# Windowed attention with block means and a squared-ReLU FFN: the first two chunks in one written order, half of the first chunk's FFN steps as three products

## The chip, the cores and the metric

The kernel runs on one core of one Trainium2 chip. The metric is the device time of one execution in microseconds. A core has TensorE (PE in the profile; its weight loads are PEld), VectorE (DVE), ScalarE (ACT), GpSimd (POOL) and SyncE (SP), which issues every DMA here. Each engine runs its own instructions in the order in which they were written; semaphores join the engines.

## The reference

Four sequences of 768 positions, eight heads of 64, then an FFN over all 3072 rows:

```
k_sum  = max  of k over blocks of 32     # 24 keys per head
v_sum  = mean of v over blocks of 32     # 24 values per head
scores = [ q k^T / 8, kept where |i - j| < 16 ;  q k_sum^T / 8 + log 32 ]
a      = softmax(scores) (sum + 1e-9)
x      = a @ [v ; v_sum]                 # heads side by side: 3072 x 512
r      = max(x @ w_in, 0)                # w_in 512 x 2048
out    = (s * r * r + b) @ w_out         # w_out 2048 x 512, s and b scalars
```

`w_in` and `w_out` come as 64-bit floats. All results are float32.

## The kernel before

**Chunks and steps.** The 3072 rows are cut into 12 chunks of 256. A chunk's attention is worked in four pairs of heads (p = 0 to 3), a pair in two halves of 128 rows. Its FFN is worked in 16 steps (f = 0 to 15): a step is 128 of the 2048 hidden units. Step f has a hidden part (`hidden`: `x @ w_in` into PSUM, 128 x 256), an activation (`activate`: ReLU and square on ACT, `s * r + b` on POOL) and a projection (`project`: two tiles of 128 x 512 that add up over the 16 steps). After the last projection `evict` copies out the chunk.

**Weights.** 32 blocks of 512 KB (an "in" and an "out" block for each step) are loaded as raw 64-bit words once. `scale_weights` (two ACT instructions a block, L118 and L119) and `convert_weights` (DVE, L132 and L134) make float32 of them. In chunk 0 the FFN multiplies in float32. From chunk 1 on, each weight, x and g is split into an upper half that TensorE multiplies in one pass and the rest (`split_weights`: upper half by ACT, lower half by DVE; `activate` splits g on DVE; `attended` splits x), and a product is the sum of three: low x high, high x low, high x high. The weights are split while chunk 0 ends, and stay.

**Attention of one pair.** `scores` (PE), `masked` (DVE: mask, scale, row minimum), `exps` (ACT), `normalize` (DVE), `transposes` (PE), `turned` (ACT copy), `values` (PE), `attended` (ACT copy). The keys and values of a window stand in one tile with 24 columns or rows of block maxima and means behind them: `fill_k` and `fill_v` copy these in (POOL, but DVE for chunk 0). In chunk 0 the scores against the maxima are a matmul of their own (`scores_of_maxima`). The means of the first sequence come from 12 matmul instructions (`mean_of_rows`, L208) against a 0-and-1/32 matrix, and `mean_done` copies them.

**Order.** Everything is written out beforehand into steps of a plan. The start, up to the first steps of chunk 0, is one written list, `FIRST_ORDER`: a letter names the function, a number its pair or step (q: keys and queries of a pair; r: rows of v; v: windows of v; i and o: weight blocks; u: keys and queries of chunk 1; W: dummy matmuls; A and B and D: scaling and converting; S, Z, M, E, N, T, C, V, X: attention; H, J, P: the three parts of an FFN step). After that, formulas place each function. The attention of chunk c lies between the FFN steps of chunk c-1. Chunk 0 takes one hidden part at a time, chunks 1 and 2 two, later ones four; the attention of chunks from 4 on is grouped (all four pairs' scores in a row, then transposes of two pairs, and so on), which `together` decides. The two scalars s and b are loaded by a DMA of their own (`load_scalars`).

**Memory.** Raw weights, split upper halves, and the first loads share 16 slots of 4 KB per partition; converted and lower weights share 33 of 2 KB. PSUM has two buffers each for hidden parts, for projections and for scores, and one each for transposes and for values.

Of the kernel before, what the change touches and what calls it, by code (L numbers as in the profile page):

```python
# [3 lines left out]

# [14 lines left out]
P = 128  # L19
# [17 lines left out]
LAG = 2  # L37
# [7 lines left out]
def windowed_attention_then_relu2_ffn(ctx, tc, qk, vwin, kt, vt, kq, vrow, wp, sb, out):  # L45
# [49 lines left out]
    mean4 = const.tile([P, KR + 20], F32, name="mean4")  # L95
    nc.gpsimd.memset(mean4, 0.0)
    nc.gpsimd.memset(mean4[:, KR - 4 : KR], 1.0 / BLOCK)
    for base, sign in ((0, 1), (BLOCK - 1, -1)):
        nc.gpsimd.affine_select(
            out=mean4[:, KR - 4 : KR], in_=mean4[:, KR - 4 : KR], compare_op=ALU.is_ge, fill=0.0,  # L100
            base=base, pattern=[[-sign * BLOCK, 4]], channel_multiplier=sign,
        )


    w_raw, w_f, w_h, w_l = {}, {}, {}, {}
# [30 lines left out]
    def split_weights(key):  # L136

        name = "_".join(map(str, key))
        whole = w_f.pop(key)
# [3 lines left out]
        nc.scalar.copy(w_h[key], whole)  # L143
        w_l[key] = wring.tile([P, 512], F32R, name=f"wl_{name}", tag="ring")
        nc.vector.tensor_tensor(
            w_l[key], whole, w_h[key].bitcast(F32), ALU.subtract
        )
# [45 lines left out]
    def load_scalars():  # L193
        nc.sync.dma_start(sb_col, sb.partition_broadcast(P))

    def keep_warm(n):

        t = ps_t.tile([P, 4 * P], F32, name="warm", tag="pt")
# [5 lines left out]
    def mean_of_rows(n):  # L204
        if n == 0:
            pm.append(ps_po.tile([P, DM], F32, name="pm", tag="po"))
        for j in (2 * n, 2 * n + 1):
            nc.tensor.matmul(  # L208
                pm[0][:KR], mean4[:, 20 - 4 * j : 20 - 4 * j + KR], vn[n][:, j % 2],
                start=(j == 0), stop=(j == 5),  # L210
            )


    vsum[0] = p2.tile([P, H, D], F32, name="vsum")

    def mean_done():
        nc.scalar.copy(vsum[0][WIN:KR].rearrange("p h d -> p (h d)"), pm[0][WIN:KR])
# [5 lines left out]
    qk_t, vw_t, ps_of, pr_of, mn_of, sm_of, pt_of, pT_of, o_of, xt = ({} for _ in range(10))  # L223
# [7 lines left out]
    def load_unit(c, p):  # L231
        t = p3.tile([P, T + NSUB * KR], F32, name="qk", bufs=4)
        nc.sync.dma_start(t, qk[c - 1, p])
        qk_t[c, p] = t[:, 0:T], t[:, T:].rearrange("p (i k) -> p i k", k=KR)
# [6 lines left out]
    def filler(c):  # L241
        return nc.gpsimd if c else nc.vector

    def fill_k(c, p):
        bi, _ = place(c)
        kw = qk_t[c, p][1]
        filler(c).tensor_copy(kw[:, :, WIN:KR], ksum[bi, p].unsqueeze(1).to_broadcast([P, NSUB, NB]))  # L247

    def fill_v(c, p):
        bi, _ = place(c)  # L250
        for e in range(2):
            filler(c).tensor_copy(  # L252
# [12 lines left out]
    def together(c):  # L265

        return c >= 4

    def scores(c, p, j):
        q, kw = qk_t[c, p]  # L270
        if j == 0:
# [5 lines left out]
            elif p == 2 and together(c):  # L277
# [64 lines left out]
    def turned(c, p):  # L342
# [4 lines left out]
        nc.scalar.copy(pT_of[c, p], pt_of.pop((c, p))[:KR])  # L347

    def values(c, p):
        vw, pT = vw_t.pop((c, p)), pT_of.pop((c, p))  # L350
# [10 lines left out]
        for i in range(NSUB):  # L361
            for e in range(2):
                oi, pi = o[64 * e : 64 * e + 64, i * SUB : (i + 1) * SUB], pT[:, e * T + i * SUB : e * T + (i + 1) * SUB]
                nc.tensor.matmul(oi, vw[:KR, e, i, :], pi, start=True, stop=True)  # L364

    def attended(c, p):
        if p == 0:
            if c == 0:
                xt[c] = (p2.tile([P, NKC, T], F32, name="x", tag="xh"),)
            else:  # L370
                xt[c] = p2.tile([P, NKC, T], F32R, name="xh", tag="xh"), p2.tile([P, NKC, T], F32R, name="xl")
        kcs = slice(p, p + (1 if c < 2 else 2))
        o = o_of.pop((c, p))[:, : (kcs.stop - p) * T].rearrange("p (k t) -> p k t", t=T)
        nc.scalar.copy(xt[c][0][:, kcs], o)
        if c > 0:
            nc.vector.tensor_tensor(xt[c][1][:, kcs], o, xt[c][0][:, kcs].bitcast(F32), ALU.subtract)


    ph_of, ph_both, gg, po = {}, {}, {}, {}

    def hidden(c, f):
        if c < 2 or f % 2 == 0:
            ph_both[0] = ps_h.tile([P, 2, T], F32, name="ph", tag="ph")
        ph = ph_of[c, f] = ph_both[0][:, f % 2]
        if c == 0:
            terms = [(w_f["in", f], xt[c][0], kc) for kc in range(NKC)]
        else:
            xh, xl = xt[c]
            terms = [
                (w["in", f], x, kc) for w, x in ((w_l, xh), (w_h, xl), (w_h, xh)) for kc in range(NKC)  # L390
            ]
# [5 lines left out]
    def activate(c, f):  # L397
        ph = ph_of.pop((c, f))
        r = p2.tile([P, T], F32, name="r")
        nc.scalar.activation(r, ph, AF.Relu)  # L400
        nc.scalar.activation(r, r, AF.Square)  # L401
        if c == 0:
            g = p2.tile([P, T], F32, name="g0", tag="gh", bufs=8)
            nc.gpsimd.tensor_scalar(g, r, s_col, b_col, ALU.mult, ALU.add)  # L404
            gg[c, f] = (g,)
            return
        g = p2.tile([P, T], F32, name="g")
        nc.gpsimd.tensor_scalar(g, r, s_col, b_col, ALU.mult, ALU.add)  # L408
# [6 lines left out]
    def project(c, f):  # L415
        if f == 0:
# [3 lines left out]
        if c == 0:  # L420
            terms = [(g[0], w_f["out", f])]
# [3 lines left out]
        for t in range(T // P):  # L425
            for n, (a, w) in enumerate(terms):
                nc.tensor.matmul(  # L427
                    po[t], a[:, t * P : (t + 1) * P], w,
                    start=(f == 0 and n == 0), stop=(f == NF - 1 and n == len(terms) - 1),
                )  # L430

    def evict(c):
        for t in range(T // P):
            o = stage.tile([P, DM], F32, name="o", tag="stage")
            nc.scalar.copy(o, po[t])  # L435
# [169 lines left out]
```

## Time and profile before

| | us |
|---|---|
| median of three runs | 636.54 (634.94 to 637.05) |
| profiled execution | 637.27 |
| its span, first to last instruction | 635.6 |
| TensorE busy | 625.9 (98%) |
| DVE / ACT / POOL busy | 310.9 / 322.1 / 183.1 |
| first projection begins | 28.72 |
| last matmul ends | 631.92 |
| mean granted clock of TensorE | 0.996 |

The profile's page gives busy time by engine and the chain of work that ended last; further views give the chain in order of time, busy time by stretch of the span, and the instructions of one engine in order of time. A row such as `36.50 1.73 PE ph L393 x8` is start, length, engine, tile written, line, and the number of instructions. A float32 matmul is two instructions. In the views of groups, the numbers behind the bar are busy time, the mean of one in ns, and the engine's idle time before them with who ended it.

### The profile page before, as it was taken

The page shows a single profiled execution, that of the slowest core. Times are in us where ns is not written, and L with a number is a line of the kernel's source. Part 1 is how long each engine was busy: PE and PEld are TensorE (multiplying, and loading weights), DVE is VectorE, ACT ScalarE, POOL GpSimd, SP SyncE. Part 2 cuts the span into 40 slices and gives each one's busy share as a digit, 9 for nine tenths or more (in the row PEclk, how much of TensorE's full clock was granted, in tenths as well). Part 3 has the DMA queues.
Part 4 walks back from the last instruction along what each step waited for, and adds up shares of the span by engine and source line. Part 5 has one row for each costly group of instructions (what it writes and reads, how often), then busy time and mean ns, then how long its engine had stood idle before and what let it go on. Part 6 is the DMA issues. An engine that isn't in the chain of part 4 may idle for free.

```text
span 635.6 us, 14057 instructions
## 1 busy us (share of the span) xinstructions
PE 625.9 (98%) x5188; PEld 548.9 (86%) x5188; DVE 310.9 (49%) x1043; ACT 322.1 (51%) x972; POOL 183.1 (29%) x352
## 2 busy tenths in 40 slices
PE   8799999999999999999999999999999999999997
PEld 6466679989899899899999998998998899899896
DVE  6786758875446245444535226245525424513311
ACT  5999867744537255336426336345346336423321
POOL 3124314323132422422151241151152142232211
PEclk9999999999999999999999999999999999999999
DMA  8999205045104113402601410700520500200000
GB/s 343 387 407 405 107 17 181 2 135 180 50 2 150 47 43 108 162 18 54 211 20 36 145 42 1 270 18 2 176 89 19 178 2 19 84 2 2 34 1 34
DMA packets 27141, 66.40 MB, mean 104 GB/s; under 512 B 3968, under 2 KB 3968, under 8 KB 27072
## 3 DMA queue, kind: packets, MB, share of 16 engines
q1 hardware_dynamic: 27072, 65.50, 29.4%
q8 instruction: 41, 0.67, 0.5%
q14 instruction: 28, 0.23, 0.1%
HBM read 59.05 MB, written 6.29 MB: 103 GB/s over the span
## 4 chain that ended last, share of the span: by engine, by line
PE 95%; DMA 4%; POOL 0%; SPq 0%; issue 0%; ACT 0%; POOLq 0%
PE po L427 43%; PE ph L393 42%; PE pav L364 4%; PE ps L290 3%; PE pt L340 3%; DMA wraw<-in_wp_dram 2%; DMA qk<-in_qk_dram 1%; DMA kq<-in_kq_dram 1%; POOL g L404 0%; SPq L228 0%; ACT o L435 0%; POOL qk L247 0%; POOLq L247 0%
## 5 line engine op out<-in xcount | busy, mean ns | idle before, releaser
L408 POOL TENSOR_SCALAR g<-r,sb_col 128x256 f32<-128x256 f32 x176 | 109.4, 622 | 365.4 <-ACT r L401 253.2
L400 ACT ACTIVATE r<-ph 128x256 f32<-128x256 f32 x192 | 72.7, 378 | 218.3 <-PE ph L393 195.7
L410 DVE CAST gh<-g 128x256 fp32r<-128x256 f32 x176 | 53.3, 303 | 247.8 <-POOL g L408 240.4
L427 PE MATMUL po<-wh,gl 128*128 128x512 f32 x352 | 141.1, 401 | 0.0
L427 PE MATMUL po<-wh,gh 128*128 128x512 f32 x352 | 138.5, 393 | 0.0
L427 PE MATMUL po<-wl_out,gh 128*128 128x512 f32 x352 | 137.4, 390 | 0.0
L393 PE MATMUL ph<-xh,wl_in 128*128 128x256 f32 x704 | 110.2, 279 | 0.0
L393 PE MATMUL ph<-xl,wh 128*128 128x256 f32 x704 | 108.6, 276 | 0.0
L393 PE MATMUL ph<-xh,wh 128*128 128x256 f32 x704 | 108.6, 276 | 0.0
L393 PEld LDWEIGHTS ph<-xh,wl_in 128*128 128x128 f32 x704 | 97.2, 188 | 5.2 <-issue 0.7
L412 DVE TENSOR_TENSOR gl<-g,gh 128x256 fp32r<-128x256 f32 x176 | 81.1, 461 | 31.2 <-PE po L427 14.7
L393 PEld LDWEIGHTS ph<-xl,wh 128*128 128x128 f32 x704 | 93.4, 188 | 0.0
L393 PEld LDWEIGHTS ph<-xh,wh 128*128 128x128 f32 x704 | 92.9, 188 | 0.0
L401 ACT ACTIVATE r<-r 128x256 f32<-128x256 f32 x192 | 80.2, 418 | 6.1
L321 ACT ACTIVATE pr<-pr,mn 128x120 f32<-128x120 f32 x176 | 67.0, 382 | 32.2 <-DVE mn L308 32.1
L427 PEld LDWEIGHTS po<-wh,gh 128*128 128x128 f32 x352 | 66.1, 188 | 14.4
L427 PEld LDWEIGHTS po<-wh,gl 128*128 128x128 f32 x352 | 66.2, 188 | 13.9 <-issue 1.4
L427 PEld LDWEIGHTS po<-wl_out,gh 128*128 128x128 f32 x352 | 66.2, 188 | 13.0
L252 POOL COPY vw<-vsum 24x256 f32<-24x256 f32 x88 | 42.2, 511 | 14.7 <-DMA vsum<-vmean 8.4
L427 PE MATMUL po<-wf_out,g 128*128 128x512 f32 x64 | 31.2, 612 | 3.1 <-POOL g L404 3.1
L435 ACT COPY o<-po 128x512 f32<-128x512 f32 x24 | 14.1, 588 | 39.1 <-PE po L427 36.6
L321 ACT ACTIVATION_READ_ACCUMULATOR pr<-pr,mn 128x1 f32 x176 | 33.0, 187 | 0.0
(70 smaller groups left out, 593.8 us busy)
## 6 DMA issues: line engine op xcount, KB each, us to landing
wraw<-in_wp_dram SPq DMA_DIRECT2D x32, 512.0 KB
qk<-in_qk_dram SPq DMA_DIRECT2D x44, 368.0 KB
vw<-in_vwin_dram SPq DMA_DIRECT2D x48, 256.0 KB
out_dram<-o SPq DMA_DIRECT2D x24, 256.0 KB
kraw<-in_kt_dram SPq DMA_DIRECT2D x12, 384.0 KB
vraw<-in_vt_dram SPq DMA_DIRECT2D x12, 252.0 KB
kq<-in_kq_dram SPq DMA_DIRECT2D x4, 512.0 KB
vraw<-in_vt_dram SPq DMA_DIRECT2D x6, 264.0 KB
```

The source lines that it names most:

```text
L252: filler(c).tensor_copy(vw_t[c, p][WIN:KR, e], vsum[bi][WIN : WIN + NB, 2 * p + e, :].unsqueeze(1).to_broadcast([NB, NSUB, D]),)
L290: nc.tensor.matmul(o, qi, kw[r, i, :], start=True, stop=True)
L321: nc.scalar.activation(pr, pr, AF.Exp, bias=mn_of[c, p][:, n : n + 1], scale=-1.0, accum_out=sm_of[c, p][:, n : n + 1])
L340: nc.tensor.transpose(pt_of[c, p][:KR, n * P : (n + 1) * P], pr[:, n, :], ident)
L364: nc.tensor.matmul(oi, vw[:KR, e, i, :], pi, start=True, stop=True)
L393: nc.tensor.matmul(ph, w[:, kc * P : (kc + 1) * P], x[:, kc], start=(n == 0), stop=(n == len(terms) - 1))
L400: nc.scalar.activation(r, ph, AF.Relu)
L401: nc.scalar.activation(r, r, AF.Square)
L408: nc.gpsimd.tensor_scalar(g, r, s_col, b_col, ALU.mult, ALU.add)
L410: nc.vector.tensor_copy(gh, g)
L412: nc.vector.tensor_tensor(gl, g, gh.bitcast(F32), ALU.subtract)
L427: nc.tensor.matmul(po[t], a[:, t * P : (t + 1) * P], w, start=(f == 0 and n == 0), stop=(f == NF - 1 and n == len(terms) - 1),)
```

## The change

- Eight FFN steps of chunk 0, f = 8 to 15 (`THREE`), are done as three products, so their weights, x and g of chunk 0 are split (`first_upper`, `first_lower`, `split_rows`). Chunk 1 takes its steps in the order 8 to 15, 0 to 7 (`SECOND`).
- Splitting a block is two functions, `upper_weights` (ACT, or DVE with a star) and `lower_weights` (DVE), each in a place of its own.
- The means: each of the six parts is four matmuls of 128 columns that write to four groups of 32 PSUM partitions, one for each pair of heads. They are not copied into chunk 0's windows: `values` multiplies the window alone and `values_of_means` adds a product with the means, whose other rows are zero.
- The scalars ride in two columns behind the first window tile of chunk 1; the load of their own is gone.
- Attention of chunks 2 and 3 is grouped as the later ones; hidden parts of chunk 2 come four at a time.
- `FIRST_ORDER` covers all of chunks 0 and 1, the attention of chunk 2 and the scores of chunk 3. Chunk 1's first scores come before chunk 0's first hidden part, and hidden parts of chunk 1 lie between the projections of chunk 0. Names now carry chunk and pair or step (`H0.9`: hidden part of step 9 of chunk 0); new letters: k and t fill windows, x loads values' windows, y takes the low part of x, Y is one of a hidden part's four products, U the means' product, F the copy of the means, G is `s * r + b`, g splits it, hi, ho, li, lo split weights, O evicts. Stars move work to the other engine: `C*`, `X*`, `hi*`, `ho*`, `G*` run on DVE; `F*` on ACT; `J*` squares on DVE, `J**` takes the maximum there, `J***` both.

```diff
-LAG = 2
...
+    THREE = (8, 9, 10, 11, 12, 13, 14, 15)
+    SECOND = THREE + tuple(f for f in range(NF) if f not in THREE)
+    def steps(c):
+        return SECOND if c == 1 else tuple(range(NF))
...
+    def upper_weights(key, other=False):
         if key[0] == "in":
             pair = slots.tile([P, 2, 512], F32R, name=f"wh_{key[1]}", tag="slot")
             w_h["in", key[1]], w_h["out", key[1]] = pair[:, 0], pair[:, 1]
-        nc.scalar.copy(w_h[key], whole)
...
+        copy(other, w_h[key], whole(key))
+    def lower_weights(key):
+        w_l[key] = wring.tile([P, 512], F32R, name="wl_" + "_".join(map(str, key)), tag="ring")
+        nc.vector.tensor_tensor(w_l[key], whole(key), w_h[key].bitcast(F32), ALU.subtract)
...
-    def load_scalars():
-        nc.sync.dma_start(sb_col, sb.partition_broadcast(P))
+    def scalars():
+        nc.gpsimd.tensor_copy(sb_col, sb_of[0])
...
         for j in (2 * n, 2 * n + 1):
-            nc.tensor.matmul(
-                pm[0][:KR], mean4[:, 20 - 4 * j : 20 - 4 * j + KR], vn[n][:, j % 2],
-                start=(j == 0), stop=(j == 5),
-            )
+            for p in range(NPAIR):
+                nc.tensor.matmul(
+                    pm[0][32 * p : 32 * p + NB], mean4[:, 20 - 4 * j : 20 - 4 * j + NB],
+                    vn[n][:, j % 2, p * P : (p + 1) * P], start=(j == 0), stop=(j == 5),
+                )
...
+    def mean_done(p, other=False):
+        dst = vsum[0][WIN:KR, 2 * p : 2 * p + 2].rearrange("p h d -> p (h d)")
+        src = pm[0][32 * p : 32 * p + NB]
+        copy(not other, dst, src)
...
     def together(c):
-        return c >= 4
+        return c >= 2
...
+    def values_of_means(p):
+        pT, o = pT_of.pop((0, p)), o_of[0, p]
+        for i in range(NSUB):
+            for e in range(2):
+                nc.tensor.matmul(
+                    o[64 * e : 64 * e + 64, i * SUB : (i + 1) * SUB], vsum[0][0:KR, 2 * p + e],
+                    pT[:, e * T + i * SUB : e * T + (i + 1) * SUB], start=False, stop=(i == NSUB - 1),
+                )
...
+                if c == 0:
+                    nc.tensor.matmul(oi, vw[0:WIN, e, i, :], pi[0:WIN], start=(i == 0), stop=False)
+                else:
+                    nc.tensor.matmul(oi, vw[:KR, e, i, :], pi, start=True, stop=True)
...
     def hidden(c, f):
+        if c == 0 and f not in THREE:
+            for kc in range(NKC):
+                hidden_part(f, kc)
+            return
+        xh, xlow = (xt["first"], xl["first"]) if c == 0 else (xt[c], xl[c])
...
+        if other < 2:
+            nc.scalar.activation(r, ph, AF.Relu)
+        else:
+            nc.vector.tensor_scalar(r, ph, 0.0, None, ALU.max)
+        if other % 2:
+            nc.vector.tensor_tensor(r, r, r, ALU.mult)
+        else:
+            nc.scalar.activation(r, r, AF.Square)
...
+        (nc.vector if other else nc.gpsimd).tensor_scalar(g, r_of.pop((c, f)), s_col, b_col, ALU.mult, ALU.add)
...
     FIRST_ORDER = (
...
+        "q1 q0 K0.1 q2 i1 S0.1.0 S0.1.1 W1 q3 Z1 K0.0 M0.1.0 S0.0.0 S0.0.1 Ai1 Z0 M0.1.1 r0 K0.2 M0.0.0 M0.0.1 "
+        "Bi1 W8 E0.0.0 S0.2.0 S0.2.1 u1.1 Z2 u1.0 K0.3 E0.0.1 r1 N0.0 k1.0 S0.3.0 S0.3.1 k1.1 E0.1.0 M0.2.0 r2 "
+        "E0.1.1 T0.0 M0.2.1 Z3 N0.1 v0 E0.2.0 C0.0 E0.2.1 v1 u1.2 i0 S1.0.0 S1.0.1 T0.1 M0.3.0 R0 M1.0.0 k1.2 "
+        "E1.0.0 o3 v2 R1 M1.0.1 N0.2 R2 E1.0.1 S1.1.0 S1.1.1 C0.1* T0.2 E0.3.0 M0.3.1 F0* M1.1.0 E0.3.1 M1.1.1 "
+        "V0.0 F1* F3 U0 N0.3 V0.1 F2 E1.1.0 v3 S1.2.0 S1.2.1 C0.2 i3 T0.3 X0.0 o2 Y1.0 E1.1.1 Ai0 N1.0 U1 M1.2.0 "
+        "V0.2 C0.3 U2 V0.3 U3 N1.1 x1.0 M1.2.1 s0 Ao3 i2 u1.3 X0.1* k1.3 T1.0 Y1.1 Bi0 X0.2 Ai3 Y1.2 o1 X0.3* Xh "
+        "Y1.3 Y0.0 Ao2 Y0.1 o0 D3 Ai2 J0.1*** C1.0* Y0.2 Y0.3 D2 H0.3 G0.1 i4 J0.0* o4 E1.2.0 Ao1 T1.1 Bo1 t1.0 "
+        "o9 Ao0 G0.0 E1.2.1 Bo0 H0.2 S1.3.0 S1.3.1 i9 Ai4 V1.0 Ao4 P0.0 J0.2** X1.0 C1.1* J0.3** Ao9 M1.3.0 x1.1 "
...
+        "G1.6 ho6* H1.4 g1.6 ho1 C2.1 T2.2 G1.2 J1.4** li5 g1.2 H1.1 H1.5 J1.1** G1.1 V2.0 lo7 C2.2* J1.5 V2.2 "
+        "V2.1 V2.3 lo6 S3.2.0 S3.2.1 k3.0 g1.1 S3.3.0 S3.3.1 S3.0.0 S3.0.1 X2.0 lo1 S3.1.0 S3.1.1 P1.1 ho4 g1.7 "
+        "X2.2 P1.2 G1.4 P1.3 y2.0 g1.4 G1.5 y2.2 g1.5 lo4"
     )
...
+    def then(step, order, fn, *args):
+        if (fn, args) not in ahead:
+            at(step, order, fn, *args)
+    for c in range(2, NC):
...
+        then(i - i % 4, HID, hidden, c, f)
+        for stage_of in (activate, scaled, split_rows):
+            then(i, CHAIN, stage_of, c, f)
+        then((i + 4) | 3, PROJ, project, c, f)
```

More of the change, by code (lines that the diff above doesn't have):

```diff
@@ L419, in project @@
         g = gg.pop((c, f))
-        if c == 0:
-            terms = [(g[0], w_f["out", f])]
+        if c == 0 and f not in THREE:
+            terms = [(g[0], whole(("out", f)))]
         else:
@@ new lines, in windowed_attention_then_relu2_ffn, with do @@
+    ahead = set()
+    def do(name):
+        how = {"other": name.count("*")} if name.endswith("*") else {}
+        name = name.rstrip("*")
+        kind = name.rstrip("0123456789.")
+        numbers = tuple(int(x) for x in name[len(kind) :].split(".") if x)
+        if kind in ("hi", "ho", "li", "lo"):
+            ahead.add((upper_weights if kind[0] == "h" else lower_weights, ((side[kind[1]], *numbers),)))
+        else:
+            ahead.add((named[kind], numbers))
+        return named[kind], numbers, how
@@ L533, in windowed_attention_then_relu2_ffn @@
[L533 to L545 removed]
+                        then(base + v_at - 5 + third, LOAD, load_v, bi, p, third)
```

279 lines of the change are left out of this document (126 added, 153 removed), and 19 rows, old and new, of the table FIRST_ORDER.

## The prediction

> **What bounds the kernel now.** I read the page's engine totals and its chain of waits first, then the chain in order of time, then the busy time by stretch, and the rows of single engines for the first 90 us.
>
> ```profile
> span 635.6 us, 14057 instructions
> ...
> PE 625.9 (98%) x5188; PEld 548.9 (86%) x5188; DVE 310.9 (49%) x1043; ACT 322.1 (51%) x972; POOL 183.1 (29%) x352
> ...
> PE 95%; DMA 4%; POOL 0%; SPq 0%; issue 0%; ACT 0%; POOLq 0%
> ```
>
> TensorE is busy for 98% of the span and makes up 95% of the chain that ended last. So time can be won in two ways only: fewer microseconds of matrix work, or less time at the start before that work is dense. The chain in order of time (start, length, what) prices the pieces:
>
> ```profile
> 36.50 1.73 PE ph L393 x8
> ...
> 40.72 1.72 PE po L427 x4
> ...
> 44.16 0.44 PE pt L340 x4
> ...
> 52.26 0.62 PE pav L364 x16
> ...
> 56.90 0.57 PE ps L290 x16
> ...
> 227.47 2.02 PE pav L364 x64
> 229.49 1.80 PE ps L290 x64
> 231.29 5.70 PE po L427 x24
> 236.99 5.47 PE ph L393 x48
> ...
> 253.42 0.87 PE pt L340 x8
> ...
> 279.11 1.80 PE ps L290 x64
> ...
> 631.92 0.59 ACT o L435
> ```
>
> The hidden part of one float32 step is the row with x8 (four products, two instructions each), 1.73 us; its projection (x4) is 1.72; 3.45 together. Four steps with three products cost 5.47 hidden and 5.50 projection (5.70 for the first after attention work), so 2.74 a step. The attention pieces of a chunk run alone cost 0.57 (scores of a pair), 0.44 (transposes), 0.62 (values); a grouped chunk costs 1.80 + 2x0.87 + 2.02 = 5.56. One chunk period is 279.11 - 229.49 = 49.62, and the last matmul ends at 631.92; 3.7 us of output follow.
>
> ```profile
> 0.00:10.00 10.00, 8.19 (x120) 7.09 (x120) 4.23 (x15) 2.98 (x10) 5.34 (x28) 1.00 0.82 306
> 10.00:21.70 11.70, 10.64 (x128) 6.51 (x124) 10.13 (x47) 10.59 (x36) 0.00 (x0) 1.00 1.01 375
> ...
> 40.00:60.00 20.00, 20.00 (x116) 13.06 (x115) 13.19 (x40) 19.81 (x52) 7.48 (x12) 1.00 1.03 405
> ```
>
> The columns of a stretch are its length, then PE, PEld, DVE, ACT and POOL busy time, granted clock, DMA share and GB/s. From 40 to 60 us TensorE has no gap while ACT is at 19.81 of 20 and DVE only at 13.19. So the first chunk is paid in float32 matrix time, ACT is full, DVE has room, and the queue of loads runs at about 405 GB/s.
>
> ```profile
> 28.72 2.71 PE L427 MATMUL po<-wf_out,g 128*128 128x512 f32 x4 [3.10 <-POOL g L404]
> ```
>
> ```profile
> 30.00:32.00 2.00, 2.00 (x14) 0.64 (x16) 1.43 (x3) 1.94 (x4) 0.00 (x0) 0.50 1.03 407
> 32.00:34.00 2.00, 2.00 (x18) 1.50 (x11) 1.53 (x11) 1.95 (x4) 0.00 (x0) 0.69 1.03 405
> ```
>
> TensorE waited 3.10 us for the first g before 28.72, and the granted clock was 0.50 and 0.69 in the four microseconds from 30: (1-0.50)x2 + (1-0.69)x2 = 1.6 us lost.
>
> **Where the two kernels become equal.** I call "the mark" the moment at which the scores of chunk 3 are done and the last four projections of chunk 1 are left. From there both kernels do the same work. In the kernel before, the like moment two chunks later is 231.29, with eight projections left. So the rest after the mark is 631.92 - 231.29 + 2x49.62 - 5.50 = 494.4 us, and the mark of before stands at 631.92 - 494.4 = 137.5. (Chunks 2 and 3 went ungrouped before; their 0.7 us each are inside 137.5 and are gone after.)
>
> **Matrix work up to the mark, part by part.** Hidden: 8 float32 steps x 1.73 and 24 steps (8 of chunk 0, 16 of chunk 1) x 1.37 = 46.7. Projection: 8 x 1.72 and 20 x 1.375 = 41.3. Before, the same were 16 x 1.73 + 16 x 1.37 and 16 x 1.72 + 12 x 1.375 = 93.6; the eight changed steps give 5.6 us back.
>
> ```profile
> L208 PE MATMUL pm<-vn,mean 128*120 128x512 f32 x12 | 5.7, 598 | 0.0
> ```
>
> The block means were 12 instructions of 128x512 for 24 useful rows, 5.7 us. They become 48 of 128 columns in four column groups. No row shows this form. A float32 instruction of 256 columns takes 1.73/8 = 0.216 us, 0.84 ns a column, so 48 x 128 columns take 5.2 us one behind the other and 1.3 four at a time: these are the bounds. The nearest row is the scores in 64x64 tiles: 16 instructions of 120 columns would take 1.6 us singly and take 0.57, nearly three at a time. I take 1.5. The means' share of the values is new matrix work: 4 x 0.62 = 2.5 by the row of values (bounds 1.7 if its two halves overlap wholly, 3.4 if not at all). It replaces eight DVE copies into the windows. Attention of chunk 0 without these: scores 2.2, maxima 1.2, transposes 1.8, values 2.5. Chunk 1: 4 x (0.57+0.44+0.62) = 6.5; chunk 2: 5.6; chunk 3's scores: 1.8. Dummy matmuls 1.9. Sum 115.4; the same sum for before is 123.3. Before, 137.5 - 123.3 = 14.2 us were not work: 9.4 before 28.72 (19.3 of the sum lie there), 1.6 of slow clock, and 3.2 in changes between unlike matmuls, which I keep for after.
>
> **The start.** Loads go out on SP's queue one behind the other.
>
> ```profile
> wraw<-in_wp_dram SPq DMA_DIRECT2D x32, 512.0 KB
> qk<-in_qk_dram SPq DMA_DIRECT2D x44, 368.0 KB
> vw<-in_vwin_dram SPq DMA_DIRECT2D x48, 256.0 KB
> ```
>
> ```profile
> 20.49 0.49 DVE L252 COPY vw<-vsum 24x256 f32<-24x256 f32 x2 [0.72 <-DMA vw<-in_vwin_dram]
> ...
> 33.29 0.42 DVE L132 TENSOR_SCALAR wf_in<-wraw 128x512 uint32<-128x512 uint32 x1
> ...
> 35.17 0.42 DVE L132 TENSOR_SCALAR wf_in<-wraw 128x512 uint32<-128x512 uint32 x1
> ...
> 61.28 0.88 DVE L134 CUSTOM_DVE_ANT_0 wf_in<-wraw,wf_in 128x1024 uint16<-128x1024 uint16 x1
> 62.08 0.68 DVE L134 CUSTOM_DVE_ANT_0 wf_out<-wraw,wf_out 128x1024 uint16<-128x1024 uint16 x1
> ```
>
> By 10 us 3.06 MB had moved (306 GB/s), and the fourth block of values, 6.29 MB deep in the queue, landed at 20.49, when 7.0 MB had moved: a load lands when about 0.7 MB more than its own depth has moved. In the new order the weights of steps 1 and 3, and two windows of chunk 1 with the scalars stand ahead: values blocks 2 and 3 are 7.16 and 7.42 MB deep, so they land at 10 + (7.42+0.7-3.06)/0.405 = 22.5. Then values, means' values and copies of pairs 2 and 3 follow until about 24.5, and hidden steps 1 and 0 until 26.2. The next hidden steps need weights:
>
> ```profile
> 57.88 0.68 ACT L118 ACTIVATE wraw<-wraw 128x512 f32<-128x512 f32 x1
> 58.46 0.66 ACT L119 ACTIVATE wraw<-wraw 128x512 int32<-128x512 uint32 x1
> 59.02 0.37 ACT L400 ACTIVATE r<-ph 128x256 f32<-128x256 f32 x1
> ```
>
> Scaling one block is 59.02 - 57.88 = 1.14 us of ACT; converting a pair is 35.17 - 33.29 = 1.88 us of DVE. Weights in_2 are 9.26 MB deep: 27.0, scaled 28.1, converted 29.5; hidden 2 ends at 31.2. Weights out_0 are 10.69 MB deep: 30.6, scaled 31.7, converted 32.7; the first projection ends at 34.4. By then 25.3 us of the work above are done (chunk 0's attention and means 11.7, four hidden steps 6.9, one projection 1.7, four scores and two transposes of chunk 1 3.1, dummies 1.9), so 9.1 us of the 34.4 are idle (9.4 before). The work pulled forward (chunk 1's scores for four pairs) goes into holes that the loads make, and later weights follow at 1.3 us each, 2.6 a step, under the 2.74 to 3.45 that a step takes: out_7 is 18.67 MB deep, 50.3, ready 53.4, against hidden 7, which has 45.2 us of matrix work ahead of it, at 45.2 + 9.1 = 54.3. That is a tie with little slack. The broadcast load of the two scalars vanishes (they ride in chunk 1's windows), and the wait of POOL behind the first window of chunk 1 with it; I count neither apart, since the loads set the times above.
>
> **Vector work.** What moves onto DVE are the weight splits (earlier), the split of x and g for eight steps, and squares, copies and maxima marked with stars.
>
> ```profile
> L412 DVE TENSOR_TENSOR gl<-g,gh 128x256 fp32r<-128x256 f32 x176 | 81.1, 461 | 31.2 <-PE po L427 14.7 <-PE ph L393 0.5 <-PE ps L290 0.5
> ...
> L410 DVE CAST gh<-g 128x256 fp32r<-128x256 f32 x176 | 53.3, 303 | 247.8 <-POOL g L408 240.4 <-PE ps L290 7.3
> ...
> L331 DVE TENSOR_TENSOR pr<-pr,rs 128x480 f32<-128x480 f32 x48 | 32.0, 666 | 1.7
> ...
> L308 DVE CUSTOM_DVE_ANT_0 pr<-ps,mask_mid 128x120 f32<-128x120 f32 x128 | 28.8, 276 | 1.1 <-PE ps L290 1.0
> ...
> L145 DVE TENSOR_TENSOR wl_in<-wf_in,wh 128x512 fp32r<-128x512 f32 x16 | 11.2, 700 | 6.4 <-ACT wh L143 6.4
> L159 DVE TENSOR_REDUCE ksum<-kraw 128x24 f32<-128x768 f32 x12 | 11.1, 940 | 0.0
> ```
>
> Start to start these are about 0.08 shorter: up to the mark 16 weight pairs x 1.88 = 30.1, 32 lower halves x 0.68 = 21.8, 24 splits of g x 0.72 = 17.3, 12 normalizations x 0.98 = 11.8, masks 48 x 0.203 = 9.8, maxima 8 x 0.87 = 7.0, the starred work and the rest 19.1: 116.9 us. ACT has 91 by like sums (32 scalings x 1.14, 24 half pairs of exponentials x 0.76, and copies and squares), POOL 30. So DVE has as much to do as TensorE and begins at 4.5 us. Each place where it waits in order (a lower half behind its upper half on ACT, a square behind its hidden step, the low part of x behind its copy) holds up everything behind it, and TensorE then waits for weights. For these, for the ties with the loads and for slow clock after gaps I allow 3 us (bounds 0 and 11).
>
> One more thing lengthens DVE's work. In DVE's rows above, the fourth and fifth are the same operation, 0.88 and 0.68 us; beside the first POOL copied values:
>
> ```profile
> 60.56 1.05 POOL L252 COPY vw<-vsum 24x256 f32<-24x256 f32 x2
> ```
>
> The Trainium skill says in SBUF — State Buffer, section Who interferes with whom, that a DVE instruction with two SBUF inputs contends with a GpSimd instruction that reads SBUF, and that who comes first holds the port for the whole instruction. By that rule, were all 30 us of POOL to block DVE, its queue would end at 4.5 + 116.9 + 30 = 151 us and the kernel at 651, an estimate; the trace agrees in kind, but with 0.2 us beside a copy of 0.5, and this outcome has its chance within rival 3.
>
> Two such rows for each of 16 copies are at most 16 x 2 x 0.2 = 6 us; they share the 3 us and its upper bound.
>
> **The sum.** 115.4 + 9.1 + 3.2 + 3 = 130.7 for the mark, against 137.5: 6.8 us less. The profiled execution took 637.27 (span 635.6 and 1.7 around it), 0.7 over the median of the runs, 636.54. 637.27 - 6.8 = 630.5.
>
> **Rivals.**
> 1. No waits beyond the start. Mark 115.4 + 9.1 + 3.2 = 127.7, 627.5; with the holes of the start filled too (idle 6.2: the first 4.5 us and 1.7 of short waits) 624.6. For it: before, TensorE ran from 28.72 without a gap. Against: then DVE had a third of its time free.
> 2. The saved matrix time is off the path. If loads, DVE and ACT together hand the pieces on no faster than before, the 5.6 us turn into waits between 34 and 90 us and the mark comes at 136 to 138: 636 to 637. For it: ACT at 19.81 of 20 and 405 GB/s before. Against: ACT's weight scaling is no longer before what TensorE needs next.
> 3. DVE becomes the bound and the kernel slower. Place: between 34 us and the mark, in DVE's queue. Price: in the stretch from 10 to 21.7 DVE with much attention work filled 10.13 of 11.70, 87%. At that fill 4.5 + 116.9/0.866 = 139.5, 2 us after the mark of before: 639. It decides from a fill below 116.9/(137.5-4.5) = 88%. For it: equal sums, in-order waits, POOL beside it. Against: ACT, when it was the bound, filled 99%.
> 4. The column groups run one behind the other. Adds 4.1 us of matrix work at 14 to 17 us, where TensorE waits for loads anyway; up to 1 us would show: 631.5.
>
> The Trainium skill, TensorE: Matmul & The Clock Gate, section Part 1, says that about 3.4 us of idle halve the clock. By it one gap of that length costs 1.7 us more; the trace agrees with 0.50 after 3.10 us.
>
> **How the numbers follow.** My forecast with rival 4: 0.60, its own range 628 to 634. Rival 1: 0.17. Rival 2: 0.12. Rival 3: 0.11. 0.3% is 1.9 us, about what a measurement here can tell from no change. Faster: 0.60 + 0.17 and a little of rival 2: 0.78; same 0.11; slower 0.11. The range reaches from rival 1 to the middle of rival 2's side: 624.5 to 636.5.
>
> **What would show it.** Eight float32 steps and 24 of three products before the mark, at 3.45 and 2.74. The first projection ending near 34. From 34 to 120 us DVE above 90% busy. TensorE idle of some 3 us after 34, released by DVE. The chunk period unchanged at 49.62. Wrong: a first projection after 38, DVE under 85% busy with TensorE idle, or idle released by loads after 45 us.

## The result and the profile after

The changed kernel takes 630.8 us (630.6 to 631.2), the one before 636.79 beside it (634.94 to 637.2): a ratio of 0.9912, 95% interval 0.9892 to 0.9933. Timed again on another occasion it took 630.83, a ratio of 0.9908 (0.9896 to 0.9921). So 5.9 us were won; 630.5 had been forecast. Of the 58 executions of the kernel before that stand beside the experiments 39 took 636.5 to 637.3 us and 13 took 634.5 to 635.5, so the gain is 6 us against the many and 4 against the few, the ratios below move with this mix, and kernels made from the changed one are held against it by their medians.

The page after: span, busy time by engine, and the shares of the chain that ended last.

```profile
span 629.2 us, 14328 instructions
...
PE 616.5 (98%) x5330; PEld 550.7 (88%) x5330; DVE 328.3 (52%) x1092; ACT 308.7 (49%) x939; POOL 187.7 (30%) x351
...
PE 87%; DVE 4%; ACT 2%; issue 1%; POOL 1%; DVEq 0%; POOLq 0%; ACTq 0%
```

TensorE has 9.4 us less to do and is still busy for 98%. What is new is the chain: TensorE falls from 95% to 87% of it, the 4% of loads are gone, and DVE and ACT are in it with 6%. The chain in order of time (start, length, what) gives the mark and what follows it:

```profile
124.92 1.80 PE ps L308 x64
126.72 4.33 PE po L488 x18
131.05 5.66 PE ph L444 x48
...
173.47 1.80 PE ps L308 x64
...
223.11 1.80 PE ps L308 x64
...
614.63 11.00 PE po L488 x48
625.66 0.59 ACT o L230
```

The scores of chunk 3 end at 126.72, three projections of chunk 1 follow (18 instructions), and at 131.05 the last four are left: this is the mark, forecast at 130.7. From it to the last matmul are 625.66 - 131.05 = 494.6 us (494.4 forecast). The period is 223.11 - 173.47 = 49.64 (49.62 before), and from the scores of chunk 5 to the last matmul it is 625.66 - 223.11 = 402.55 after and 631.92 - 229.49 = 402.43 before. So everything was won ahead of the mark.

Busy time by stretch (length, PE, PEld, DVE, ACT, POOL, granted clock, DMA share, GB/s):

```profile
0.00:20.00 20.00, 13.70 (x284) 11.58 (x286) 13.85 (x67) 11.72 (x49) 6.59 (x33) 1.00 0.91 349
20.00:34.00 14.00, 13.24 (x172) 10.59 (x170) 13.26 (x38) 13.98 (x36) 2.62 (x5) 1.00 1.03 414
34.00:60.00 26.00, 25.65 (x164) 17.12 (x164) 25.41 (x62) 24.78 (x56) 13.28 (x14) 1.00 1.03 418
60.00:82.00 22.00, 20.34 (x157) 17.39 (x150) 20.01 (x45) 20.37 (x44) 8.97 (x9) 1.00 0.55 213
82.00:100.00 18.00, 17.90 (x150) 16.00 (x151) 16.77 (x61) 12.32 (x38) 7.08 (x13) 1.00 0.08 22
100.00:120.00 20.00, 20.00 (x123) 17.64 (x122) 18.26 (x44) 7.88 (x25) 5.44 (x10) 1.00 0.30 99
```

TensorE is idle for 6.3 us up to 20, 0.8 up to 34, and 0.35 + 1.66 + 0.10 = 2.1 after that. DVE is at 80.45 of 86 us from 34 to 120, 93.5%. From 20 to 82 us three engines stand close to full side by side. The rows of TensorE that the forecast spoke of, in order of time:

```profile
4.20 0.92 PE L311 MATMUL ps<-kq 64*64 64x96 f32 x16 [4.20 <-DMA kq<-in_kq_dram]
...
7.41 3.14 PE L208 MATMUL warm<-ones 128*128 128x128 f32 x16
10.47 0.56 PE L311 MATMUL ps<-kq 64*64 64x96 f32 x16
...
15.79 1.79 PE L217 MATMUL pm<-vn,mean 128*24 128x128 f32 x48
...
34.74 3.67 PE L488 MATMUL po<-wf_out,g 128*128 128x512 f32 x8 [0.26 <-DVE wf_out L141]
...
81.88 0.71 PE L444 MATMUL ph<-x0h,wl_in 128*128 128x256 f32 x4 [1.38 <-DVE wl_in L155]
```

The first projection is half of the row at 34.74, so it ends near 36.6. The longest wait after it is 1.38 us, for a lower half from DVE.

### The profile page after: what moved, and what is told of

It reads as the page before. It is cut to its first block, busy times and chain, and to the rows that moved or that the text cites. A ratio compares the mean times of both kernels' runs of the same rounds, so it can differ in the third digit from the quotient of the medians.

```text
span 629.2 us, 14328 instructions
## 1 busy us (share of the span) xinstructions
PE 616.5 (98%) x5330; PEld 550.7 (88%) x5330; DVE 328.3 (52%) x1092; ACT 308.7 (49%) x939; POOL 187.7 (30%) x351
## 4 chain that ended last, share of the span: by engine, by line
PE 87%; DVE 4%; ACT 2%; issue 1%; POOL 1%; DVEq 0%; POOLq 0%; ACTq 0%
PE po L488 40%; PE ph L444 38%; PE pav L394 3%; PE pt L358 3%; PE ps L308 3%; DVE wf_out L141 1%; POOL g L466 1%; DVE wl_in L155 1%; DVE wf_in L141 0%; DVE wf_in L139 0%; ACT r L458 0%; DVE wf_out L139 0%; ACT wraw L125 0%; ACT wraw L126 0%; ACT r L452 0%
## 5 line engine op out<-in xcount | busy, mean ns | idle before, releaser
L466 POOL TENSOR_SCALAR g<-r,sb_col 128x256 f32<-128x256 f32 x189 | 127.1, 673 | 379.2 <-ACT r L458 256.0
L452 ACT ACTIVATE r<-ph 128x256 f32<-128x256 f32 x179 | 67.6, 378 | 206.1 <-PE ph L444 187.0
L488 PE MATMUL po<-wh,gl 128*128 128x512 f32 x368 | 146.3, 397 | 0.0
L488 PE MATMUL po<-wh,gh 128*128 128x512 f32 x368 | 145.0, 394 | 0.0
L488 PE MATMUL po<-wl_out,gh 128*128 128x512 f32 x368 | 144.2, 392 | 0.0
L473 DVE TENSOR_TENSOR gl<-g,gh 128x256 fp32r<-128x256 f32 x184 | 85.8, 466 | 33.6 <-PE po L488 16.4
L458 ACT ACTIVATE r<-r 128x256 f32<-128x256 f32 x184 | 77.0, 418 | 15.2 <-DVE r L454 9.7
L488 PEld LDWEIGHTS po<-wh,gh 128*128 128x128 f32 x368 | 69.2, 188 | 14.3
L488 PEld LDWEIGHTS po<-wl_out,gh 128*128 128x128 f32 x368 | 69.2, 188 | 13.8
L349 DVE TENSOR_TENSOR pr<-pr,rs 128x480 f32<-128x480 f32 x48 | 32.0, 666 | 1.7
```

What stands on the lines that cost most here:

```text
L349: nc.vector.tensor_tensor(pr, pr, rs.unsqueeze(2).to_broadcast([P, 4, KR]), ALU.mult)
L466: (nc.vector if other else nc.gpsimd).tensor_scalar(g, r_of.pop((c, f)), s_col, b_col, ALU.mult, ALU.add)
L473: nc.vector.tensor_tensor(gl, g, gh.bitcast(F32), ALU.subtract)
L488: nc.tensor.matmul(po[t], a[:, t * P : (t + 1) * P], w, start=(f == steps(c)[0] and n == 0), stop=(f == steps(c)[-1] and n == len(terms) - 1),
```

## The experiments

### What each part is worth

**The three products.** `SPLIT_FIRST` replaces `THREE` wherever chunk 0 asks which form a step takes, and the places of the splits in the list follow.

```diff
+    SPLIT_FIRST = ()
...
-        if c == 0 and f not in THREE:
+        if c == 0 and f not in SPLIT_FIRST:
```

> The kernel after, but all 16 steps of chunk 0 multiply in float32: the split of x and of g for chunk 0 is gone, and the lower halves of steps 8 to 15 come right behind the last float32 use of their block. Nothing is left out. Theory A (TensorE's work sets the mark): 8 x 0.69 = 5.5 us more matrix work, of which up to 1.5 us fills holes: 634.8 to 636.3, and the mark near 135 to 136.5. Rival B (DVE and ACT set the pace until 82 us, where the chain of waits runs through them): DVE has 1.2 + 8 x 0.72 = 7.0 us less to do, and the saving of the three products shows in part: 632 to 633.5.

Measured: 633.97 us (633.47 to 634.74), ratio 0.9965 (0.9955 to 0.9975). The three products are worth 3.2 us, not the 5.6 of matrix work. Its busy time by stretch, against the rows of the changed kernel from 34 us on:

```profile
34.00:60.00 26.00, 25.75 (x142) 16.75 (x142) 23.57 (x58) 23.79 (x53) 10.33 (x14) 1.00 1.03 417
60.00:82.00 22.00, 21.96 (x142) 16.16 (x135) 17.45 (x35) 19.55 (x42) 7.72 (x9) 1.00 0.52 204
82.00:100.00 18.00, 18.00 (x126) 13.76 (x125) 13.85 (x52) 12.49 (x39) 6.83 (x14) 1.00 0.08 23
```

With float32 alone TensorE is idle for 0.3 us from 34 to 100, against 2.1: 1.8 us of the saving turn into waits. A second part goes in the steps themselves. In the changed kernel the first four matmuls of a three-product hidden step of chunk 0 are mostly slower than the next four:

```profile
61.30 0.74 PE L444 MATMUL ph<-x0h,wl_in 128*128 128x256 f32 x4
61.88 0.64 PE L444 MATMUL ph<-x0l,wh 128*128 128x256 f32 x4
62.35 0.64 PE L444 MATMUL ph<-x0h,wh 128*128 128x256 f32 x4
```

From 61.30 to 0.48 after 62.35 it takes 1.53 us where I had put 1.37. Read in the same way, the eight steps take 1.44 to 1.63 us each, 1.2 us more than forecast in all: 5.6 - 1.8 - 1.2 = 2.6, and the two profiled spans differ by 631.8 - 629.2 = 2.6.

**The column groups.** The means again as 12 matmuls of 512 columns; all else stays.

```diff
-            for p in range(NPAIR):
-                nc.tensor.matmul(pm[0][32 * p : 32 * p + NB], ..., vn[n][:, j % 2, p * P : (p + 1) * P], ...)
+            nc.tensor.matmul(pm[0][:NB], ..., vn[n][:, j % 2], ...)
```

> The kernel after, with the block means as 12 float32 instructions of 512 columns again (24 rows out, no column groups); the copies per pair of heads and the product with the means stay. Nothing is left out. The means then take about 5.6 us of TensorE instead of the 1.8 us measured. Theory A (TensorE waits in the first 34 us for ACT and DVE anyway): within 0.7 us of the kernel after, 630.3 to 631.5. Rival B (the means stand in TensorE's queue ahead of chunk 0's transposes, so the whole start shifts): 2 to 4 us more, 633 to 635.

Measured: 633.42 us (633.16 to 635.38), ratio 0.9958 (0.9947 to 0.997).

```profile
15.37 5.33 PE L216 MATMUL pm<-vn,mean 128*24 128x512 f32 x12
...
37.32 1.96 PE L487 MATMUL po<-wf_out,g 128*128 128x512 f32 x4 [0.26 <-DVE wf_out L141]
```

The means take 5.33 us instead of 1.79, the first projection comes at 37.32 instead of 34.74, and the whole 2.6 us arrive at the end. So the means lie on the path that sets the start.

**The dummy matmuls.** `W1` and `W8` are struck from the list.

> The kernel after without its 18 dummy matmul instructions (3.1 us at 7.4 to 10.5 us and 0.8 us at 5). They feed no output. Theory A (the start is set by ACT and DVE): within 0.5 us of the kernel after, 630.3 to 631.3. Rival B (they hold TensorE's clock up): float32 pieces between 11 and 25 us take up to twice as long, first projection 1 to 3 us later, 632 to 634. Rival C (they stand in front of the scores of pair 2 and delay them): first projection up to 1 us earlier, 630.

Measured: 631.95 us (631.46 to 632.48), ratio 0.9936 (0.9919 to 0.9953): 1.1 us slower.

```profile
13.04 1.08 PE L358 MATMUL pt<-ident,pr 128*120 128x128 f32 x4 [1.36 <-DVE pr L349]
...
16.52 2.37 PE L217 MATMUL pm<-vn,mean 128*24 128x128 f32 x48
18.82 0.64 PE L308 MATMUL ps<-qk 64*64 64x120 f32 x16
19.39 0.65 PE L358 MATMUL pt<-ident,pr 128*120 128x128 f32 x4
```

```profile
14.00:16.00 2.00, 2.00 (x36) 1.65 (x36) 1.57 (x10) 1.49 (x7) 0.11 (x1) 1.00 1.03 401
```

The four transposes take 1.08 us at 13.04 and 0.65 at 19.39: TensorE runs slow until about 18 us, though the granted clock (third from the end in the last row, the stretch from 14 to 16) reads 1.00. The first projection comes at 35.59.

**The fill that POOL waited for, in the kernel before.** `G0`, the copy of the maxima into chunk 1's first window, moves behind `J1` in the list of the kernel before; nothing else changes.

```diff
-X2 B2 V3 X3 G0 H0 i5 A3 B3 H1 J0 P0 o5 A4 A5 J1 A6 A7
+X2 B2 V3 X3 H0 i5 A3 B3 H1 J0 P0 o5 A4 A5 J1 G0 A6 A7
```

> The kernel before, with one name moved in its written list: POOL's fill of the first window of chunk 1 (G0) goes behind the activation of step 1, so the first g no longer stands behind a load. Nothing is left out. Theory A (of the gain of 6.0 us, the part at the start is the wait of 3.10 us in front of the first projection plus the 1.6 us of clock 0.50 and 0.69 after it): first projection near 26, clock 1.00 throughout, 4.7 us less at most: 632 to 633.5. Rival B (the weights are late next: step 2 is converted at 27 to 28 us in any case, so most of the wait only moves): first projection near 26 but a gap before step 2 or 3, less than 2 us gained: 635 or more.

Measured: 635.09 us (634.88 to 635.82) against 636.63 for the kernel before beside it, ratio 0.9986 (0.9977 to 0.9995).

```profile
26.82 1.99 PE L427 MATMUL po<-wf_out,g 128*128 128x512 f32 x4
30.34 0.64 PE L290 MATMUL ps<-qk 64*64 64x120 f32 x16 [1.54 <-POOL qk L247]
```

The wait of 3.10 us ahead of the first projection is gone and it begins at 26.82, but chunk 1's scores now wait 1.54 us for the same fill. The gain is 0.9 us by the ratio and 1.5 by the medians, at most half of the wait. What the wait alone was worth stays open: in this profiled execution the granted clock was 0.50 from 11.1 to 14.5 us, which costs 1.7 us ahead of the first projection, where the kernel before had its 1.6 us of slow clock behind it.

### What sets the start

**Fewer loads.** Two of the three loads of rows are left out (1.05 MB ahead of the weights) and the first block serves for all three.

```diff
+        if j > 0:
+            vn[j] = vn[0]
+            return
```

> The kernel after; only the first of the three 512 KB row loads for the block means is made and used three times (the means are wrong; 1.05 MB, 2.6 us of the load queue, are left out). Theory A, the one of the forecast (the loads set the first projection at 34.7): it comes 1.5 to 2.6 us earlier, 628.2 to 629.5. Rival B (ACT and DVE, both full from 20 to 34 us, and TensorE's queue set it; the wide means cost 2.6 us there): first projection within 0.5 us of 34.7 and the time within 0.7 us of 630.8.

Measured: 630.63 us (630.34 to 632.89), ratio 0.9925 (0.9899 to 0.9952), the same time as the changed kernel.

```profile
34.57 3.67 PE L491 MATMUL po<-wf_out,g 128*128 128x512 f32 x8 [0.26 <-DVE wf_out L141]
```

The queue of loads did run ahead: a group of eight weight loads that SP begins to issue at 28.39 us in the changed kernel begins at 26.04. The first projection still begins at 34.57 instead of 34.74, and in four other runs with the same start it begins between 34.28 and 34.61. Loads do not set it.

**An earlier start for ACT.** The exponentials of pair 1 go ahead of the first scaling, the dummies to the very front of TensorE, and DVE's order follows.

```diff
-q1 q0 ... S0.0.1 Ai1 Z0 M0.1.1 r0 K0.2 M0.0.0 M0.0.1 Bi1 W8 E0.0.0 S0.2.0 ...
+W8 q1 q0 ... S0.0.1 Z0 M0.1.1 E0.1.0 E0.1.1 Ai1 r0 K0.2 M0.0.0 M0.0.1 E0.0.0 S0.2.0 ...
```

> Order of the start alone: the exponentials of pair 1 of chunk 0 (four at 0.38 us each, 1.5 us of ACT) go ahead of the scaling of the first weights, into the time in which ACT now stands idle until 9.34 us; pair 1 then goes ahead of pair 0 through normalization and transposes, the dummy matmuls go to the very front of TensorE's queue, and the masking of pair 2 moves up on DVE ahead of the first conversion. Theory A (in the first 35 us the queue of ACT and DVE hands the pieces on): the first projection begins at 33.3 to 34.2 instead of 34.74, and the time falls by as much, to 629.4 to 630.3 us. Theory B (loads set the start after all, or the new order only moves the wait): the first projection stays at 34.5 to 35, 630.8 us. If TensorE, idle between the early dummies and the first transposes, runs slower again as it did without the dummies, the time rises to 631.5 to 632.

Measured: 632.91 us (632.7 to 633.78), ratio 0.9942 (0.993 to 0.9955), 2.1 us slower than the changed kernel beside it. ACT did begin at 6.67, but TensorE then stood still from 6.8 to 9.3. Its busy time by stretch, with the granted clock third from the end:

```profile
7.00:8.00 1.00, 0.00 (x0) 0.00 (x0) 0.60 (x5) 1.00 (x7) 0.45 (x3) 1.00 0.95 320
8.00:9.00 1.00, 0.00 (x0) 0.00 (x0) 1.00 (x6) 0.39 (x3) 0.00 (x0) 0.66 1.05 410
9.00:10.00 1.00, 0.70 (x15) 0.73 (x19) 0.93 (x7) 1.00 (x2) 0.00 (x0) 0.50 0.99 406
...
18.00:19.00 1.00, 1.00 (x36) 0.86 (x25) 0.93 (x4) 1.00 (x7) 0.00 (x0) 0.72 1.05 427
19.00:20.00 1.00, 1.00 (x30) 0.68 (x19) 1.00 (x6) 0.98 (x6) 0.37 (x2) 1.00 1.00 397
```

The clock was halved from 8.3 to 18.6 us. The clock hides what the order alone would bring; that stays open. In the changed kernel the dummies at 7.41 stand where the gap would be.

### What sets the pace from 34 to 100 us

**Less matrix work.** The product low x high is left out of chunk 0's eight split steps (7.3 us of TensorE).

```diff
+ ... ((w_l, xh), (w_h, xh)) if c == 0 else ((w_l, xh), (w_h, xlow), (w_h, xh))
...
+            if c == 0:
+                terms = terms[1:]
```

> The kernel after; the eight split steps of chunk 0 take two of the three products (low x times high weights and low g times high weights are left out in chunk 0, so its results are a little less exact). All DVE and ACT work stays. TensorE has 8 x (4 + 2) instructions less: 8 x 0.92 = 7.3 us of matrix work between 49 and 100 us. Theory A (from 34 us to the mark TensorE sets the pace, DVE close behind): 3 to 6 us less, 625 to 628. Rival B (the chain through DVE and ACT sets the pace there; the saving of the three products showed at 3.2 of 5.5 us for this reason): less than 2.5 us, 628.3 to 630.8, and the missing part is TensorE's idle time released by DVE.

Measured: 630.73 us (630.56 to 631.6), ratio 0.9924 (0.9899 to 0.9949): nothing won.

```profile
34.00:60.00 26.00, 24.73 (x152) 16.00 (x148) 25.41 (x62) 24.99 (x56) 11.10 (x14) 1.00 1.03 417
60.00:82.00 22.00, 17.25 (x117) 13.90 (x117) 20.03 (x45) 19.86 (x43) 9.00 (x9) 0.99 0.53 208
82.00:100.00 18.00, 17.40 (x141) 15.61 (x141) 16.93 (x62) 12.92 (x40) 6.97 (x13) 0.92 0.09 26
```

TensorE's idle time from 34 to 100 grows from 2.1 to 6.6 us, and DVE and ACT are about as full as they were. Of the waits of TensorE that the trace names between 60 and 90 us ACT releases most, the longest among them (2.17 us before 81.89), and not DVE as the rival had it. Around that wait the clock is 0.50 from 81.6 to 85.0 us, which costs another 1.7. So 4.5 of the 7.3 us turn into waits, and without the slow clock perhaps 1.7 us would have been won. TensorE alone doesn't set the pace there.

**Less DVE work.** Of the sixteen lower halves of the in-weights one is computed and stands for all, so fifteen subtractions, 10 us of DVE, are left out.

```diff
+        if ("in" in [k[0] for k in w_l] if key[0] == "in" else False):
+            whole(key)
+            w_l[key] = next(w for k, w in w_l.items() if k[0] == "in")
+            return
```

> The kernel after; the lower half of an 'in' block is made for one step alone and used for all (the other 15 subtractions of 0.68 us on DVE are left out, 10.2 us; results less exact). Theory A (after 34 us TensorE sets the pace and waits for DVE only some 2 us): 1 to 2.5 us less, 628.3 to 629.8. Rival B (DVE is the bound up to the mark): 5 us or more less, 625.8 or below.

Measured: 628.34 us (627.48 to 628.86), ratio 0.988 (0.9859 to 0.9902): 2.5 us faster than the changed kernel by the medians.

```profile
60.00:82.00 22.00, 21.96 (x179) 19.59 (x171) 18.32 (x42) 21.06 (x45) 9.32 (x11) 1.00 0.54 203
82.00:100.00 18.00, 17.89 (x147) 15.84 (x146) 15.02 (x59) 13.44 (x43) 6.78 (x14) 1.00 0.19 56
```

The gap of 1.66 us between 60 and 82 is 0.04, and from 34 to 120 us TensorE is idle for 0.7 us instead of 2.1. That is 1.4 of the 2.5 us; where the rest lies was not told apart. With DVE relieved, TensorE sets the pace again. So theory A holds: of ten microseconds of DVE's work no more than 2.5 were in TensorE's way.

**More ACT work.** The stars of all `J` are taken away: 7.3 us of maxima and squares go from DVE to ACT.

> The kernel after with all stars of the activations taken off: the 13 maxima and 8 squares that ran on DVE run on ACT (7.3 us moved). Nothing is left out. Theory A (DVE is the tighter of the two after 34 us, ACT has 91 of some 125 us): within 1 us, 629.8 to 631.8. Rival B (ACT, full until 60 us with the scaling of weights, hands on later): first 20 us after 34 grow, 2 to 4 us more, 632.8 to 634.8.

Measured: 634.13 us (633.18 to 634.53), ratio 0.9971 (0.9959 to 0.9982): 3.3 us slower by the medians.

```profile
34.00:60.00 26.00, 25.82 (x142) 16.32 (x141) 23.52 (x57) 25.54 (x61) 8.48 (x13) 1.00 1.03 418
60.00:82.00 22.00, 20.69 (x188) 18.09 (x187) 18.93 (x42) 21.74 (x46) 7.18 (x10) 1.00 0.58 211
82.00:100.00 18.00, 16.71 (x142) 14.79 (x141) 16.31 (x60) 14.14 (x44) 7.58 (x14) 1.00 0.08 22
```

From 60 to 82 us ACT is now at 21.74 of 22 and DVE at 18.93, where the changed kernel has 20.37 and 20.01: the stars keep the two level. Part of the loss comes earlier, since the first projection begins at 35.55, 0.8 us later.

**POOL as the helper.** POOL has room, so two kernels try to give it DVE's work.

```diff
-        nc.vector.tensor_tensor(w_l[key], whole(key), w_h[key].bitcast(F32), ALU.subtract)
+        eng = nc.gpsimd if key in (("out", 8), ("out", 9), ("out", 10), ("out", 11)) else nc.vector
+        eng.tensor_tensor(w_l[key], whole(key), w_h[key].bitcast(F32), ALU.subtract)
```

> Four lower halves (the output weights of steps 8 to 11) are subtracted by POOL instead of DVE, 4 x 0.61 = 2.4 us off DVE between 59 and 76 us, where POOL is busy 9 of 22 us. Theory A (DVE's queue sets the pace in this stretch; leaving out ten microseconds of it gave 2.5): TensorE's gap of 1.7 us between 60 and 82 us shrinks by 0.6 to 1, 629.8 to 630.2 us. Theory B (POOL takes longer for them than its own scalings of g can wait, or slows DVE beside it): the gaps are no smaller, 630.8 to 632 us.

Measured: 632.24 us (631.88 to 634.37), ratio 0.9936 (0.9923 to 0.9948), 1.4 us slower; TensorE's idle time from 34 to 100 us is 4.2 us instead of 2.1.

```diff
-            nc.vector.tensor_tensor(r, r, r, ALU.mult)
+            eng = nc.gpsimd if (c, f) in ((0, 0), (0, 1)) else nc.vector
+            eng.tensor_tensor(r, r, r, ALU.mult)
...
-        nc.vector.tensor_tensor(xl["first"], xt[0], xt["first"].bitcast(F32), ALU.subtract)
+        nc.gpsimd.tensor_tensor(xl["first"], xt[0], xt["first"].bitcast(F32), ALU.subtract)
```

> Three pieces of DVE's work go to POOL at places where POOL stands idle: the squares of steps 1 and 0 of chunk 0 (at 28.4 and 31.7 us, 0.34 us of DVE's queue each) and the lower half of x for chunk 0 (at 47.2 us, 1.13 us of the queue). That is 1.8 us off DVE before 60 us; ACT, TensorE and the loads keep all they have. Theory A (DVE's queue, full from 10 us on, sets the pace, as leaving out ten microseconds of lower halves said with 2.5 us): the first projection begins at 34.1 instead of 34.74 and the time is 629.0 to 630.4 us, against 630.83 for the changed kernel. Theory B (ACT, full from 20 to 60 us, holds the pieces back as much, so that DVE alone gives nothing, or POOL hands its pieces on later than DVE did): the first projection at 34.6 or later and 630.6 to 631.5 us.

Measured: 632.02 us (631.6 to 632.56), ratio 0.9926 (0.9913 to 0.994), 1.2 us slower, with the first projection at 34.86. The reason is in the rows of the second kernel: POOL's, then DVE's beside it, then TensorE's.

```profile
42.96 2.54 POOL L419 TENSOR_TENSOR x0l<-xh,x0h 128x1024 fp32r<-128x1024 f32 x1
```

```profile
43.19 2.85 DVE L141 CUSTOM_DVE_ANT_0 wf_in<-wraw,wf_in 128x1024 uint16<-128x1024 uint16 x1
45.97 0.68 DVE L141 CUSTOM_DVE_ANT_0 wf_out<-wraw,wf_out 128x1024 uint16<-128x1024 uint16 x1
```

```profile
49.28 1.97 PE L427 MATMUL ph<-xh,wf_in 128*128 128x256 f32 x8 [1.19 <-DVE wf_in L141]
```

The conversion takes 2.85 us instead of 0.68; it ends 0.54 us after POOL's subtraction, which ended at 45.50. DVE was to be relieved of 1.13 us here and stood for 2.2 instead, and TensorE waits 1.19 for the weights. In the first of the two kernels the same shows four times, once with a plain cast, which took 303 ns in the mean in the kernel before:

```profile
78.31 1.28 POOL L156 TENSOR_TENSOR wl_out<-wf_out,wh 128x512 fp32r<-128x512 f32 x1
```

```profile
78.38 1.36 DVE L472 CAST gh<-g 128x256 fp32r<-128x256 f32 x1 [0.47 <-POOL g L467]
```

None of these kernels that computes the whole beats the changed one. The changed kernel itself, timed beside the early ACT and the lower halves on POOL, took 630.83 us (630.08 to 631.41); its expectation was:

> The changed kernel itself once more, with nothing edited, timed beside the next two so that each stands against it on one chip. Every theory: 630.8 us as before (630.6 to 631.2), 5.3 to 6 us under the kernel before. If it comes out 1 us away, the earlier comparisons between calls are worth no more than that.

## Why the prediction was right, point by point

**The total, right; two of its terms wrong in opposite directions.** To the end of the first projection I had 34.4; it was 36.6, 2.2 late. From there to the mark I had 96.3; 131.05 - 36.6 = 94.45, 1.85 less. That the two cancel to within 0.35 us at the mark is luck, but for one piece that stands in both: the values of chunk 1's first pair, 0.6 us, run ahead of the first projection, and I had counted them behind it. Most of the rest of the later part is waits, some 1.85 us instead of 3.

**The start: the step "loads set the times" was wrong.** With 1.05 MB less ahead of the weights that I had taken for the bound, the first projection moved by 0.17 us; with means 3.5 us longer, by 2.6. From 20 to 34 us TensorE is busy for 13.24 of 14 us, DVE for 13.26, ACT for 13.98. There are no holes made by loads for the pulled-forward work to fall into. That ACT, the fullest of the three, hands the pieces on is argued from these figures and not shown: the run that was to show it was spoiled by the clock. TensorE's real idle time to the end of the first projection is 7.3 us, less than my 9.1; what I had short, by 4 us, is its work: the sixteen dummies at 7.41 take 3.14 (1.9 for all eighteen in the sum), the first scores 0.92 instead of 0.57, the means 1.79 instead of 1.5, and the values just named were missing. For the dummies and the first scores I had taken later, faster rows as prices, though TensorE runs slow there: the same scores take 0.56 at 10.47.

**The column groups: mechanism right, cover wrong.** 1.5 us were forecast, 1.79 measured. The rival on them said that a serial form would show "up to 1 us", since TensorE waits for loads there. The wide form, close to it in length, shows the whole 2.6: the named cover does not exist.

**The three products: 5.6 us of work, 3.2 of time.** The work was rightly counted but for the slower first products (1.2 us over the eight steps). The waits that come with it are the 3 us of my sum, measured as 2.1; the two rows shown, 0.26 and 1.38 us, are released by DVE, as was to be seen.

**Rival 2, in part.** The next saving of matrix time is off the path for the most part, as the two-product kernel shows: 7.3 us less work won nothing, 4.5 of them for waits and 1.7 for the slow clock behind one. The changed kernel stands where TensorE, DVE and ACT are about equal from 34 to 82 us.

**Rival 3.** It did not come about: DVE holds TensorE up from 34 to 82 us, but only by about 2 us (ten microseconds off it give 2.5, where a DVE that bounds alone would have given 5 or more), and its filling is 93.5%, above the 88% under which the rival would decide. The rival's price of an 87% fill was read off the stretch from 10 to 21.7, which was no measure for the later one. Why DVE fills better there was not tried apart.

**POOL beside DVE.** I weighed a rule by which one of them holds the other up for a whole instruction, and gave it no more than the 0.2 us per operation that the trace of before showed. The experiments with longer POOL instructions show the full block: 2.85 us beside one of 2.54, 1.36 beside 1.28. This is what the Trainium skill says in SBUF — State Buffer, section Who interferes with whom: where a DVE instruction in its two-port mode meets one of GpSimd, who issues first has the shared ports for the whole instruction, and the other is blocked and not slowed; these rows agree.

**The equality after the mark and the period:** held, with 49.64 against 49.62 us. The slow clock that the sum left out is gone too: from 20 us on no stretch of the changed kernel shown here is under 1.00.

## What to carry to other kernels

Ask of a saved microsecond which engine is next to full in the same stretch: here 5.6 us of TensorE bought 3.2, and the following 7.3 bought nothing (some 1.7 of them went in a slow clock). A start that looks bound by loads has to be tested by taking a load away, and its pieces priced from rows of the start. An idle POOL is no free hand for DVE's work on SBUF: what it takes over, it can take from DVE twice.

## What the runs showed of the hardware

- During a gap of 2.5 us in TensorE's early work (6.8 to 9.3, in the kernel with the early ACT) the clock fell to half at 8.3 us and stayed there until 18.6, though work began again at 9.3. Waits of 0.60 and 1.04 us close together came before half the clock in the experiment on the fill (11.1 to 14.5), and one of 2.17 went with it in the two-product kernel (81.6 to 85.0); one of 1.74 us at 13.34 in the changed kernel was not followed by slow rows. Half the clock lasted 3.4 us in these two cases and in the kernel before (29.9 to 33.3), and 10.2, three times as long, in the kernel with the early ACT, where TensorE worked without a gap only from 15.0 us on. The Trainium skill, TensorE: Matmul & The Clock Gate, section Part 1, gives about 3.4 us as the idle window and as much of sustained work to come back; the way back agrees, and for the way down less idle time than that was enough.
- The column of the granted clock can read 1.00 while TensorE is slow: in the kernel without dummies it does from 14 to 16 us, between transposes of 1.08 us at 13.04 and means of 2.37 at 16.52, which take 0.65 and 1.79 elsewhere. The clock record of that trace opens only at 18.3 us, with the full clock. Early on, the durations are to be believed.
- 48 float32 matmuls in four column groups took 1.79 us, against 5.33 for the same sums in 12 wide ones: three times as fast.
- The first four matmuls of a three-product hidden step took 0.58 us start to start at 61.30, 0.11 more than the next four. It is not the float32 work ahead of them alone: at 73.00 and 75.99 they took 0.58 behind matmuls of their own kind, after their weight loads had waited 0.19 and 0.39 us for ACT, and at 83.39, behind a step like theirs, 0.48.
